# One chunk of LN2's modulation on GpSimd, the shared chunk last in Wo, two K steps moved up, fewer warm-ups: a DiT block on one core

## The chip, the cores and the metric

The kernel runs on one core of a Trainium2 chip (trn2). The metric is the device time of one execution in microseconds (us). The kernel before took 244.13 us, the median of three executions (243.96 to 244.31). An execution counts as slow when it is over 1.5% longer than the fastest of the same kernel; all others are called fast, and only fast ones are compared. In what follows PE is TensorE (the matmul engine), ACT is ScalarE, DVE is VectorE, POOL is GpSimd and SP is SyncE, which issues most DMAs.

## The reference

A DiT block with modulated layer norms, attention with two heads of 576 and a four-fold MLP, all in bfloat16.

```python
B, N, D, F = 2, 256, 1152, 4608
mod = (silu(c) @ w_mod).reshape(B, 6, 1, D)
shift_a, scale_a, gate_a, shift_m, scale_m, gate_m = [mod[:, i] for i in range(6)]
h = layernorm(x) * (1 + scale_a) + shift_a
q, k, v = split(h @ wqkv)                      # H = 2, Dh = 576
a = softmax(q @ k.T * Dh ** -0.5) @ v          # per head
x = x + gate_a * (a.reshape(B, N, D) @ wo)
h2 = layernorm(x) * (1 + scale_m) + shift_m
return x + gate_m * (gelu(h2 @ w_fc1) @ w_fc2)
```

The 512 tokens are four tiles of 128 (tiles 0 and 1 are batch 0, tiles 2 and 3 batch 1). D is nine chunks of 128 columns. A head has four and a half chunks, so chunk 4 (`HC = Dh // P`) is shared by the two heads.

## The kernel before

Four places matter. Each engine gets its instructions in the order in which the program writes them, which is the order here. `P` is 128, `N` the 256 tokens of a batch, `T` all 512; `KM1` is 6. The "K stage" below is the K projection with what feeds it.

The start. PE has nothing real to do until x has been normalised, so it multiplies zeros ("warm-ups") to get its clock up (in the trace of before the step from one to the next falls from 427 to 216 ns). Then it transposes normalised x, computes `scale_a` in four groups of columns (`scale_group`, waits for parts of `w_mod`), has ACT or DVE multiply the transposed x by it (`modulate`), and starts the K projection one contraction chunk at a time (`k_step`), on whichever tiles are ready.

```python
def k_step(k, c0=0, c1=T):              # six output chunks, contraction chunk k, tokens c0:c1
    for m in range(KM1):
        ...
        nc.tensor.matmul(pk[m][:, c0:c1], w_k[:, k, m * P:(m + 1) * P], hT0[:, k, c0:c1], ...)

warm(18, pwarm)                         # after 4 earlier ones
act_stats(ACT.Identity, dsum)
...
norm1(0, 0, CUT, "d")                   # tile 0 normalised, by DVE
pt_0 = transpose_x([0, 1], [0])
warm(3, pwarm)
...
scale_group(0)("a")                     # PE: scale of chunks 0, 1; ACT: + 1
for k in range(2): modulate(pt_0, k, k, 0, 0, P, "a")
warm(1, pwarm)
pt_1 = transpose_x([0, 1], [1])
for k in range(2): modulate(pt_1, k, k, 1, 0, P, "d")
...
pt_2 = transpose_x([0, 1], [2])
for k in range(2): modulate(pt_2, k, k, 2, 0, P, "a")
scale_group(1)("a")
sqrt1(3); recip1(3)
norm1(3, 0, CUT, "d")                   # tile 3 normalised
pt_3 = transpose_x([2, 3], [0, 1])
for i, k in enumerate((2, 3)): modulate(pt_3, i, k, 0, 0, N, "a")
k_step(0, N, N + P)                     # tile 2's first K steps
k_step(1, N, N + P)
pt_4 = transpose_x([0, 1], [3])
for k in range(2): modulate(pt_4, k, k, 3, 0, P, "d")
k_step(2, 0, N)
k_step(3, 0, N)
...
pt_5 = transpose_x([2, 3], [2, 3])
```

The loads that feed this part are issued in this order by SP, right behind x.

```python
KGROUPS = [(0, 2), (2, 4), (4, 6), (6, 9)]
for k0, k1 in KGROUPS:
    nc.sync.dma_start(w_scale_a[:, :, k0 * P:k1 * P], wmod_v[...])    # scale weights of the group
    for k in range(k0, k1):
        nc.sync.dma_start(w_k[:, k, 0:KM1 * P], wqkv_v[...])          # K weights, chunk by chunk
```

The Wo projection contracts over the nine chunks of `aT`, which ACT and DVE have just copied from PSUM; the shared chunk 4 is copied last (`pv_shared`).

```python
for k in range(KD):                     # KD = 9
    nc.tensor.matmul(pacc[:], aT[:, k, t * P:(t + 1) * P], w_o[:, k, c0:c1], start=(k == 0), stop=(k == KD - 1))
```

LN2's modulation works in place on `hT`, which a transposing DMA writes. FC1 (`w_f1`) of batch 0 starts on it chunk by chunk.

```python
def ln2_modulate(b, ks=range(KD)):
    for k in ks:
        h = hT[:, k, b * N:(b + 1) * N]
        if b == 0 or k % 3 == 2:
            nc.scalar.activation(h, h, ACT.Identity, bias=shift_m[...], scale=scale_m[...])
        else:
            nc.vector.tensor_scalar(h, h, scale_m[...], shift_m[...], op0=ALU.mult, op1=ALU.add)
...
wo_group(3, 0)
ln2_modulate(0, range(6))
ln2_stats(2, 2)
ln2_sqrt(2)
ln2_modulate(0, range(6, KD))
wo_group(3, 1)
...                                     # then FC1
```

Of the kernel before, what the change touches and what calls it, by code (L numbers as in the profile page):

```python
# [11 lines left out]
ALU = mybir.AluOpType  # L12
# [7 lines left out]
def kernel(  # L20
# [11 lines left out]
    nc = tc.nc  # L32
    B, N, D = x.shape
# [3 lines left out]
    P = 128  # L37
# [3 lines left out]
    KD = D // P  # L41
# [17 lines left out]
    def acc_tile(shape, name, dt=FP32):  # L59
        return psum.tile(shape, dt, name=name, tag="acc", bufs=6)  # L60

    def aux_tile(shape, name, dt=FP32):
        return psum.tile(shape, dt, name=name, tag="aux", bufs=2)
# [95 lines left out]
    HC = Dh // P  # L159
# [4 lines left out]
    pwarm = acc_tile([P, T], "pwarm")  # L164


    def warm(n, dst):
        for _ in range(n):
            nc.tensor.matmul(dst[:], zeros[:, 0:P], zeros[:], start=True, stop=True)  # L169
# [30 lines left out]
    def act_stats(f, dst):  # L200
        nc.scalar.activation(
            xns[T_ACT][:], x_sb[:, T_ACT, :], f, bias=pivot, scale=-1.0, accum_out=dst[:],
        )

    def act_stats_finish():
        nc.vector.scalar_tensor_tensor(
            dm2[:], dsum[:], -1.0 / (D * D), dsum[:], op0=ALU.mult, op1=ALU.mult
        )
        nc.vector.scalar_tensor_tensor(
            mv1[:, T_ACT, 1:2], dsq[:], 1.0 / D, dm2[:], op0=ALU.mult, op1=ALU.add  # L210
        )
        nc.vector.scalar_tensor_tensor(
            mv1[:, T_ACT, 0:1], dsum[:], -1.0 / D, pivot, op0=ALU.mult, op1=ALU.add
        )
# [4 lines left out]
    def recip1(t, with_nb=False):  # L219
        nc.vector.reciprocal(rstd1[:, t:t + 1], rstd1[:, t:t + 1])  # L220
        if with_nb:
            nc.vector.scalar_tensor_tensor(
                nb1[:, t:t + 1], mv1[:, t, 0:1], -1.0, rstd1[:, t:t + 1], op0=ALU.mult, op1=ALU.mult
            )

    def norm1(t, c0, c1, eng):
        if eng == "a":
            nc.scalar.activation(
                xns[t][:, c0:c1], x_sb[:, t, c0:c1], ACT.Identity,
                bias=nb1[:, t:t + 1], scale=rstd1[:, t:t + 1],  # L230
            )
        else:
            nc.vector.tensor_scalar(
                xns[t][:, c0:c1], x_sb[:, t, c0:c1], mv1[:, t, 0:1], rstd1[:, t:t + 1],
                op0=ALU.subtract, op1=ALU.mult,
            )
# [23 lines left out]
    def transpose_x(ks, ts, pt=None, js=None):  # L260
        pt = aux_tile([P, len(ks), len(ts) * P], "pt", BF16) if pt is None else pt
        for i, k in enumerate(ks):
            for j, t in enumerate(ts) if js is None else zip(js, ts):
                nc.tensor.transpose(pt[:, i, j * P:(j + 1) * P], xns[t][:, k * P:(k + 1) * P], ident[:])
        return pt

    def modulate(pt, i, k, t0, j0, w, eng):
        b = t0 // TPB
        dst, src, sc = hT0[:, k, t0 * P:t0 * P + w], pt[:, i, j0:j0 + w], scale_a[:, k, b:b + 1]
        if eng == "d":  # L270
            nc.vector.tensor_scalar_mul(dst, src, sc)
        else:
            nc.scalar.mul(dst, src, sc)
# [8 lines left out]
    def k_step(k, c0=0, c1=T):  # L282
        for m in range(KM1):
            if k == 0 and c0 == 0:
                pk[m] = acc_tile([P, T], "pk")
            nc.tensor.matmul(  # L286
                pk[m][:, c0:c1], w_k[:, k, m * P:(m + 1) * P], hT0[:, k, c0:c1],
                start=(k == 0 and c0 == 0), stop=(k == KD - 1), skip_group_check=True,
            )
# [36 lines left out]
    s_rows = work.tile([P, KD, SW], BF16, name="s_rows", tag="s_rows", bufs=1)  # L326

    CUT = 4 * P
    warm(18, pwarm)
    act_stats(ACT.Identity, dsum)  # L330
    for j in range(NPD):
        stats_piece(0, j)
# [4 lines left out]
    norm1(0, 0, CUT, "d")  # L337
    stats_piece(2, 1)
    pt_0 = transpose_x([0, 1], [0])
    warm(3, pwarm)  # L340
    act_stats_finish()
    sqrt1(T_ACT)
    stats_piece(2, 2, False)
# [24 lines left out]
    sqrt1(3)  # L368
    recip1(3)
    norm1(3, 0, CUT, "d")  # L370
    pt_3 = transpose_x([2, 3], [0, 1])
    for i, k in enumerate((2, 3)):
        modulate(pt_3, i, k, 0, 0, N, "a")
    k_step(0, N, N + P)
    k_step(1, N, N + P)
    pt_4 = transpose_x([0, 1], [3])
    for k in range(2):
        modulate(pt_4, k, k, 3, 0, P, "d")
# [33 lines left out]
    def vec_section(stat, w, name, nk=KD):  # L412
        pn = aux_tile([P, nk * 32], "pn")
        for k in range(KD):
            wk4 = w[:, k, :].rearrange("p (j q r) -> p q j r", q=4, r=32)
            for i in range(4):
                nc.tensor.matmul(
                    pn[32 * i:32 * i + SW, :].rearrange("p (j r) -> p j r", r=32),
                    stat[:, k, :], wk4[:, i, :, :],
                    start=(k == 0), stop=(k == KD - 1), tile_position=(0, 32 * i),  # L420
                )
        dst = act.tile([P, nk, 32], FP32, name=name)
        nc.vector.transpose(dst[:].rearrange("p k c -> p (k c)"), pn[:])
        return dst
# [59 lines left out]
    scale_m = act.tile([P, KD, B], FP32, name="scale_m")  # L484
# [8 lines left out]
    for k in range(KD):  # L493
        for m in range(KM1):
            nc.tensor.matmul(  # L495
                pq[m][:], w_q[:, k, m * P:(m + 1) * P], hT[:, k, :],
                start=(k == 0), stop=(k == KD - 1),
            )
    for m in range(KD):
        if m >= KM1:  # L500
            pq.append(acc_tile([P, T], "pacc"))
            for k in range(KD):
                nc.tensor.matmul(
                    pq[m][:], w_q[:, k, m * P:(m + 1) * P], hT[:, k, :],
                    start=(k == 0), stop=(k == KD - 1),
# [10 lines left out]
    for b in range(B):  # L516
        for h in range(H):
            scores[b, h] = acc_tile([P, TPB, N], "ps_s")
            for qt in range(TPB):
                q0 = b * N + qt * P  # L520
                for i in range(HC):
# [3 lines left out]
                        start=(qt == 0 and i == 0), stop=False, skip_group_check=True,  # L525
                    )
    for b in range(B):
        for qt in range(TPB):
            q0 = b * N + qt * P
            for h in range(H):  # L530
# [3 lines left out]
                    start=False, stop=True, skip_group_check=True, tile_position=(h * HP, 0),  # L534
# [128 lines left out]
    def ln2_modulate(b, ks=range(KD)):  # L663
        for k in ks:
            h = hT[:, k, b * N:(b + 1) * N]
            if b == 0 or k % 3 == 2:
                nc.scalar.activation(  # L667
                    h, h, ACT.Identity, bias=shift_m[:, k, b:b + 1], scale=scale_m[:, k, b:b + 1],
                )
            else:  # L670
                nc.vector.tensor_scalar(
                    h, h, scale_m[:, k, b:b + 1], shift_m[:, k, b:b + 1], op0=ALU.mult, op1=ALU.add,
                )
# [5 lines left out]
    def wo_group(t, i):  # L679
        b = t // TPB  # L680
        c0, c1 = cuts[t][i:i + 2]
        pacc = acc_tile([P, c1 - c0], "pacc")
        for k in range(KD):
            nc.tensor.matmul(  # L684
                pacc[:], aT[:, k, t * P:(t + 1) * P], w_o[:, k, c0:c1],
                start=(k == 0), stop=(k == KD - 1),
            )
        tmp = work.tile([P, c1 - c0], FP32, name="tmp", tag="tmp", bufs=3)
        nc.vector.tensor_tensor(tmp[:], pacc[:], gate_a[:, b, c0:c1], op=ALU.mult)  # L689
        (nc.vector if (t, i) in ((1, 2), (3, 3)) else nc.gpsimd).tensor_tensor(  # L690
            x1[:, t, c0:c1], tmp[:], x_sb[:, t, c0:c1], op=ALU.add
        )

    def ln2_stats(t, i):
        c0, c1 = cuts[t][i:i + 2]
        nc.vector.bn_stats(stats2[t][:, i, :], x1[:, t, c0:c1])

    wo_group(0, 0)
    wo_group(0, 1)
    ln2_stats(0, 0)  # L700
    wo_group(0, 2)
    ln2_stats(0, 1)
    wo_group(1, 0)
# [19 lines left out]
    shift_m = vec_section(sT, w_shift_m, "shift_m")  # L723
# [4 lines left out]
    ln2_stats(2, 1)  # L728
# [6 lines that stand above are left out]
    ln2_stats(3, 0)  # L735
# [52 lines left out]
    for b in range(B):  # L788
        for m0 in range(0, MSPLIT, 2):
            ms = range(m0, min(m0 + 2, MSPLIT))  # L790
            pacc = acc_tile([P, len(ms), N], "pacc")
            for m in ms:
                for k in range(KD):
                    f1_mm(pacc[:, m - m0, :], m, k, b * N, (b + 1) * N)
            if b == 0 and ms[-1] == MSPLIT - 3:
                ln2_modulate(1)
            nc.scalar.activation(gT[:, ms[0]:ms[-1] + 1, b * N:(b + 1) * N], pacc[:], ACT.Gelu_apprx_tanh)  # L797
# [41 lines left out]
    for gi, (n, t, c0, cw) in enumerate(groups):  # L839
        b = t // TPB  # L840
        last = gi == len(groups) - 1
        pacc = acc_tile([P, cw], "pacc")
        for kk in range(KF):
# [4 lines left out]
                start=(kk == 0), stop=(kk == KF - 1),  # L848
# [51 lines left out]
```

## Time and profile before

| what | before |
|---|---|
| median of 3 executions | 244.13 us |
| profiled span | 242.5 us |
| PE busy | 237.0 us, 98% |
| sum of PE's losses in the K stage, 9.7 to 14.3 us | 1.4 us |
| loss in the first Wo group | 0.14 us |
| loss at the start of FC1 | 0.52 us |

From the page of the kernel before, two rows of the table of engines (busy us, share of the span, instructions) and the first line of the chain of waits that ended last:

```profile
PE 237.0 (98%) x1703; PEld 143.4 (59%) x1703; DVE 93.2 (38%) x207; ACT 70.7 (29%) x141; POOL 31.3 (13%) x47
PE 58%; ACT 2%; DMA 1%; issue 0%; DVE 0%; ACTq 0%; DVEq 0%
```

PE is the engine that counts. But 98% busy doesn't mean that it lost nothing in between. Matmuls overlap in the trace, so the end of one covers the start of the next (the profile's page lists those of Wo at 314 ns in the mean, while one of 384 columns starts every 163). The Trainium skill warns of the busy share in "Perfetto Trace Analysis", section "Identifying the Most-Contended Engine": it is not a good measure of how close to its peak TensorE runs, because its instructions are pipelined. That 98% also hides waits is what this trace adds. The view of PE's waits names few of them (who waited for whom: us in total, times, longest us):

```profile
PE pwarm L169 <- DVE eps_t L92: 1.2, 1, 1.2
PE pt L264 <- ACT big L273: 0.3, 1, 0.3
PE pacc L781 <- ACT hT L667: 0.2, 1, 0.2
```

Apart from the start it names 0.5 us. Subtracting from each matmul's start the start of the one before, and comparing that with the step of an unhindered stream in this trace (216 ns for 512 columns, 163 for 384, 109 for 256, 56 for 128), finds 2.1 us: 1.4 in the K stage, 0.14 in Wo, 0.52 at FC1. (Ten switches from one kind of matmul to another, of 0.09 to 0.11 us each, are left out.) This count of lost step time is what the rest of the document uses. (A few matmul records are missing from a trace; they show as exactly two steps and are not losses.)

The K stage in the timeline of before (start us, length us, engine, line, operation, out<-in, how many in a row, idle before and what ended it; some lines between are left out here and in the fences below):

```profile
3.14 5.54 PE L169 MATMUL pwarm<-zeros 128*128 128x512 bf16 x18
8.52 0.28 PE L264 MATMUL pt<-ident,xn 128*128 128x128 bf16 x2
9.28 0.59 PE L246 MATMUL pm<-sT,w_scale_a 128*128 128x2 bf16 x18
10.60 0.47 DVE L271 TENSOR_SCALAR big<-pt,scale_a 128x128 bf16<-128x128 bf16 x2 [1.46 <-ACT big L273]
13.12 0.38 PE L264 MATMUL pt<-ident,xn 128*128 128x128 bf16 x4 [0.29 <-ACT big L273]
13.34 0.83 PE L286 MATMUL pk<-big,w_k 128*128 128x128 bf16 x12
13.82 0.41 DVE L233 TENSOR_SCALAR xn<-x_sb,mv,rstd 128x512 bf16<-128x512 bf16 x1
14.29 0.28 PE L264 MATMUL pt<-ident,xn 128*128 128x128 bf16 x2
14.41 1.47 PE L286 MATMUL pk<-big,w_k 128*128 128x256 bf16 x12
```

The transposes of tile 0 (8.52) come straight after the last warm-up; their input had been ready since 7.14. The first scale group follows at 9.28; its weights had landed at 8.77. At 13.12 the transposes `pt_3` wait for ACT, then tile 2's K steps run (13.34), and then `pt_4` starts at 14.29, just after DVE has normalised tile 3 (13.82 + 0.41).

The start of Wo and of FC1 in the same timeline:

```profile
77.07 9.10 PE L684 MATMUL pacc<-w_o,big 128*128 128x384 bf16 x54
77.23 0.58 ACT L298 CAST big<-pa 128x512 bf16<-128x512 f32 x1 [0.47 <-PE pa L619]
94.51 3.06 ACT L667 ACTIVATE hT<-hT,shift_m,scale_m 128x256 bf16<-128x256 bf16 x6 [3.41 <-DMA hT<-xn]
97.65 1.57 ACT L667 ACTIVATE hT<-hT,shift_m,scale_m 128x256 bf16<-128x256 bf16 x3
97.88 1.17 PE L781 MATMUL pacc<-hT,w_f 128*128 128x256 bf16 x8
99.27 3.98 PE L781 MATMUL pacc<-hT,w_f 128*128 128x256 bf16 x35 [0.22 <-ACT hT L667]
```

Chunk 4's copy ends at 77.81, while the fifth matmul of Wo could have run at 77.73. ACT gets the nine chunks of batch 0 done at 99.22; FC1 wants the eighth at 98.64 and the ninth 0.11 us later.

### The profile page before, as it was taken

The numbers are of one execution on the slowest core, as the hardware profiler recorded it, in microseconds if no ns is written. First come the engines' busy times: TensorE is split into PE (matmuls) and PEld (weight loads), VectorE is DVE, ScalarE is ACT, GpSimd is POOL, SyncE is SP. The second block draws the span as 40 slices with busy tenths as digits, with TensorE's granted clock in tenths as the row PEclk, the third lists the DMA queues.
The fourth block names the chain that finished last, engine by engine and source line by source line (L and its number), as shares of the span: only waits on it lengthen the run. The fifth ranks groups of instructions, "written<-read, shape, count | busy, mean of one in ns | idle before, by whom it ended". The sixth has DMA issues, their size and how long they took to land.

```text
span 242.5 us, 4040 instructions
## 1 busy us (share of the span) xinstructions
PE 237.0 (98%) x1703; PEld 143.4 (59%) x1703; DVE 93.2 (38%) x207; ACT 70.7 (29%) x141; POOL 31.3 (13%) x47
## 2 busy tenths in 40 slices
PE   8999999999999999999999999999999999999994
PEld 2586444466656566888854444444665666566573
DVE  3762550665694676720000029999001000000001
ACT  6542250543736074872222223332000000000000
POOL 1012000000310516200000000000314111111111
PEclk9999999999999999999999999999999999999999
DMA  7999999999999998789999999997981000000000
GB/s 238 329 334 343 383 356 224 351 367 275 256 322 364 377 248 213 188 193 332 328 328 254 212 232 326 327 327 220 281 255 35 16 16 16 19 19 27 21 17 16
DMA packets 76989, 54.48 MB, mean 225 GB/s; under 512 B 26011, under 2 KB 72491, under 8 KB 76971
## 3 DMA queue, kind: packets, MB, share of 16 engines
q1 hardware_dynamic: 76240, 53.02, 77.4%
q0 software_dynamic: 704, 1.20, 1.6%
q8 instruction: 13, 0.21, 0.4%
q14 instruction: 5, 0.04, 0.0%
q10 hardware_dynamic: 27, 0.00, 0.0%
HBM read 46.90 MB, written 1.19 MB: 198 GB/s over the span
## 4 chain that ended last, share of the span: by engine, by line
PE 58%; ACT 2%; DMA 1%; issue 0%; DVE 0%; ACTq 0%; DVEq 0%
PE pacc L845 29%; PE pacc L781 29%; ACT hT L667 2%; DMA hT<-xn 1%; ACT xn L650 0%; ACT rstd L641 0%; DVE tmp L851 0%; DVE o_sb L853 0%; ACTq L667 0%; DVEq L851 0%
## 5 line engine op out<-in xcount | busy, mean ns | idle before, releaser
L781 PE MATMUL pacc<-hT,w_f 128*128 128x256 bf16 (+1 forms) x432 | 70.7, 326 | 0.2 <-ACT hT L667 0.2
L845 PE MATMUL pacc<-w_f,gT 128*128 128x384 bf16 (+2 forms) x468 | 70.5, 314 | 0.0
L845 PEld LDWEIGHTS <-gT 128*128 128x128 bf16 x468 | 44.4, 98 | 26.2
L781 PEld LDWEIGHTS <-w_f 128*128 128x128 bf16 x432 | 42.2, 98 | 28.2 <-issue 0.5
L469 DVE SCALAR_TENSOR_TENSOR late<-w_gate_mT,late 128x1152 bf16<-128x1152 bf16 x18 | 24.4, 1357 | 36.8 <-DMA w_gate_mT<-in_w_mod_dram 36.2
L851 DVE TENSOR_TENSOR tmp<-pacc,gate 128x384 f32<-128x384 f32 (+2 forms) x13 | 6.8, 526 | 63.0 <-PE pacc L845 51.3
L819 ACT ACTIVATE gT<-pacc 128x512 bf16<-128x512 f32 x24 | 14.3, 597 | 32.3 <-PE pacc L781 32.3
L469 DVE SCALAR_TENSOR_TENSOR s_spill<-w_scale_m,s_b 128x1152 bf16<-128x1152 bf16 x12 | 16.3, 1357 | 8.3 <-DMA w_scale_m<-in_w_mod_dram 8.0
L684 PE MATMUL pacc<-w_o,big 128*128 128x384 bf16 (+2 forms) x117 | 18.1, 314 | 0.0
L568 PE MATMUL pacc<-w_v,hT 128*128 128x384 bf16 x108 | 17.9, 326 | 0.0
L853 POOL TENSOR_TENSOR o_sb<-tmp,x 128x384 bf16<-128x384 f32 (+1 forms) x12 | 11.6, 972 | 48.1 <-DVE tmp L851 48.1
L684 PEld LDWEIGHTS <-big 128*128 128x128 bf16 x117 | 10.9, 98 | 7.0 <-ACT big L298 0.4
L568 PEld LDWEIGHTS <-hT 128*128 128x128 bf16 x108 | 10.4, 98 | 7.0 <-issue 0.2
L286 PE MATMUL pk<-big,w_k 128*128 128x128 bf16 (+2 forms) x102 | 13.4, 279 | 0.1
L690 POOL TENSOR_TENSOR x<-tmp,x_sb 128x384 f32<-128x384 f32 (+1 forms) x11 | 9.8, 889 | 18.0 <-DVE tmp L689 9.3
L495 PE MATMUL pacc<-hT,w_q 128*128 128x512 bf16 x54 | 11.8, 379 | 0.0
L324 POOL DMA_DIRECT2D gates_dram<-grow x4 | 2.0, 514 | 70.6 <-DVE grow L805 70.6
L797 ACT ACTIVATE gT<-pacc 128x512 bf16<-128x512 f32 x12 | 6.9, 597 | 10.8 <-PE pacc L781 10.8
L169 PE MATMUL pwarm<-zeros 128*128 128x512 bf16 x26 | 8.6, 486 | 1.2 <-DVE eps_t L92 1.2
L286 PEld LDWEIGHTS <-w_k 128*128 128x128 bf16 x102 | 7.8, 98 | 3.1 <-issue 0.2
L495 PEld LDWEIGHTS <-w_q 128*128 128x128 bf16 x54 | 5.3, 98 | 6.4
L689 DVE TENSOR_TENSOR tmp<-pacc,gate 128x384 f32<-128x384 f32 (+2 forms) x13 | 6.7, 522 | 5.5 <-PE pacc L684 5.4
(98 smaller groups left out, 160.2 us busy)
## 6 DMA issues: line engine op xcount, KB each, us to landing
w_f<-in_w_fc_dram SPq DMA_DIRECT2D x14, 864.0 KB, 10.9
w_f<-in_w_fc_dram SPq DMA_DIRECT2D x2, 2592.0 KB, 10.3
w_f<-in_w_fc_dram SPq DMA_DIRECT2D x2, 1728.0 KB, 14.5
w_shift_a<-in_w_mod_dram SPq DMA_DIRECT2D x3, 864.0 KB, 11.0
w_v<-in_wqkv_dram SPq DMA_DIRECT2D x3, 864.0 KB, 6.0
w_gate_a<-in_w_mod_dram SPq DMA_DIRECT2D x3, 864.0 KB, 9.1
w_o<-in_wo_dram SPq DMA_DIRECT2D x3, 864.0 KB, 6.0
w_shift_m<-in_w_mod_dram SPq DMA_DIRECT2D x3, 864.0 KB, 13.0
```

Source lines behind the costliest of these rows:

```text
L169: nc.tensor.matmul(dst[:], zeros[:, 0:P], zeros[:], start=True, stop=True)
L286: nc.tensor.matmul(pk[m][:, c0:c1], w_k[:, k, m * P:(m + 1) * P], hT0[:, k, c0:c1], start=(k == 0 and c0 == 0), stop=(k == KD - 1), skip_g ...
L469: nc.vector.scalar_tensor_tensor(spill, wT[:, j, :], 1.0, s_b[b], op0=ALU.mult, op1=ALU.mult, accum_out=dst(j, b),)
L495: nc.tensor.matmul(pq[m][:], w_q[:, k, m * P:(m + 1) * P], hT[:, k, :], start=(k == 0), stop=(k == KD - 1),)
L568: nc.tensor.matmul(pacc[:], hT[:, k, t * P:(t + 1) * P], w_v[:, k, pnl * PW:(pnl + 1) * PW], start=(k == 0), stop=(k == KD - 1),)
L684: nc.tensor.matmul(pacc[:], aT[:, k, t * P:(t + 1) * P], w_o[:, k, c0:c1], start=(k == 0), stop=(k == KD - 1),)
L690: (nc.vector if (t, i) in ((1, 2), (3, 3)) else nc.gpsimd).tensor_tensor(x1[:, t, c0:c1], tmp[:], x_sb[:, t, c0:c1], op=ALU.add)
L781: nc.tensor.matmul(dst, w_f1[m // KD][:, k, ml * P:(ml + 1) * P], hT[:, k, c0:c1], start=(k == 0), stop=(k == KD - 1),)
L797: nc.scalar.activation(gT[:, ms[0]:ms[-1] + 1, b * N:(b + 1) * N], pacc[:], ACT.Gelu_apprx_tanh)
L819: nc.scalar.activation(gT[:, m, :], pacc[:], ACT.Gelu_apprx_tanh)
L845: nc.tensor.matmul(pacc[:], gT[:, kk, t * P:(t + 1) * P], w_f2[j][:, r, c0 - n * PW:c0 - n * PW + cw], start=(kk == 0), stop=(kk == KF - 1),)
L853: (nc.vector if last else nc.gpsimd).tensor_tensor(o_sb[:], tmp[:], x1[:, t, c0:c0 + cw], op=ALU.add)
```

## The change

Four small things. Fewer warm-ups should let the transposes of tile 0 start when their input is ready. Tile 2's first K steps go ahead of the transposes `pt_3`, to fill PE's wait at 13 us. The shared chunk goes last in Wo's contraction, so that its copy has time. The last chunk of batch 0's LN2 modulation goes from ACT to POOL, so that the chain of nine on ACT becomes eight.

```diff
-    warm(18, pwarm)
+    warm(12, pwarm)
...
     pt_0 = transpose_x([0, 1], [0])
-    warm(3, pwarm)
+    warm(4, pwarm)
...
     norm1(3, 0, CUT, "d")
+    k_step(0, N, N + P)
+    k_step(1, N, N + P)
     pt_3 = transpose_x([2, 3], [0, 1])
     for i, k in enumerate((2, 3)):
         modulate(pt_3, i, k, 0, 0, N, "a")
-    k_step(0, N, N + P)
-    k_step(1, N, N + P)
     pt_4 = transpose_x([0, 1], [3])
...
-            if b == 0 or k % 3 == 2:
+            if b == 0 and k == KD - 1:
+                nc.gpsimd.tensor_scalar(
+                    h, h, scale_m[:, k, b:b + 1], shift_m[:, k, b:b + 1], op0=ALU.mult, op1=ALU.add,
+                )
+            elif b == 0 or k % 3 == 2:
                 nc.scalar.activation(
...
-        for k in range(KD):
+        ks = [k for k in range(KD) if k != HC] + [HC]
+        for k in ks:
             nc.tensor.matmul(
                 pacc[:], aT[:, k, t * P:(t + 1) * P], w_o[:, k, c0:c1],
-                start=(k == 0), stop=(k == KD - 1),
+                start=(k == ks[0]), stop=(k == ks[-1]),
```

## The prediction

> **What bounds it now.** TensorE. The page gives PE 237.0 of 242.5 us busy (98%), and the chain of waits is two PE stages, FC1 and FC2 (29% each), reached through ACT modulations of batch 0's LN2. Busy hides small stalls, so I compared the starts of successive matmuls with their streaming step (216 ns for 512 columns, 109 for 256, 56 for 128). Apart from the cold start and fixed switches of about 0.1 us, PE loses time in three places only:
> - K stage, 9.7 to 14.3 us: five waits, 0.27+0.29+0.16+0.43+0.28 = 1.4 us, for ACT and DVE results.
> - First Wo group, 77.7 us: chunk 4 waits 0.14 us for the shared chunk's ACT copy (77.23 to 77.81).
> - FC1 start, 98.6 to 99.3 us: chunks 7 and 8 wait 0.14+0.38 us for ACT, which modulates nine chunks in line, about 0.5 us each, after the transposing DMA landed at 94.40.
>
> After 14.3 us PE is fed without further stalls, and the DMA landings I checked have 0.7 us or more of slack, so time won early should reach the end.
>
> **Warm-ups.** In the timeline their step is 427 ns until 6.1 us, then 216: seven of the 18 are cold. The Trainium skill, "TensorE: Matmul & The Clock Gate", Part 1, says the ramp is a time of activity (about 3.4 us), not a count; this trace agrees roughly (matmuls from 1.2 us, warm at 6.1). So the six removed are warm: 6 x 0.216 = 1.3 us, and one added back, 0.2. But the first transposes then run at 7.2 instead of 8.5 us, and the modulation products behind them need the first scale weights, which land at 8.77 us. They start now at 9.28, so they can move to about 8.85: a gain of 0.35 to 0.4, not 1.1. About 0.6 us of new PE idle appears before them. The next scale group has its weights at 11.85 (used at 12.2), just early enough.
>
> **K steps ahead of the transposes.** They fill the 0.43 us wait. But from 10.6 us the chain that ends last is DVE: modulate, statistics, normalize of tile 3 (10.60 to 14.23), then the transposes at 14.29. PE only waits sooner or later for it. Worth about 0 by itself (-0.1 to +0.15).
>
> **Shared chunk last.** The first Wo group reads chunk 4 at 8 x 0.163 = 1.3 us after its start, well after the copy. Gain 0.14.
>
> **Chunk 8 on GpSimd.** It leaves the ACT queue (0.5 us less) and runs on POOL between two additions, about 96.7 us. POOL's two-input 128x384 addition takes 0.91 us; the skill's "GPSIMD Engine Reference", section 4.1, calls one-input work roughly line-rate; no such instruction is in this trace. I estimate 0.4 to 0.8 us, done before 97.6, needed at 98.7. The 0.38 wait goes; chunk 7's 0.14 stays, since ACT's start and PE move together. Gain 0.38.
>
> **Sum.** 0.37 + 0 + 0.14 + 0.38 = 0.9 us: 244.13 becomes **243.2 us**, 80% range 242.8 to 243.65. Faster by over 2%: 0.005; within 2%: 0.985; slower by over 2%: 0.01.
>
> **Right if:** pt_0's transposes near 7.2 us; scale group 0 waits on its DMA and starts near 8.85; tile 3's transposes near 13.9; no wait inside the first Wo group; FC1's last-chunk wait on ACT gone with one of about 0.14 at chunk 7; K stage done about 0.4 us earlier.
>
> **Wrong if:** the clock warms later in the new schedule or drops again in the new idle gap (slower by 1 us or more); the scale weights land earlier or later than profiled (each 0.1 us counts fully until the K stage); GpSimd's instruction takes over 2 us; or the reordered K steps push the next transposes and ACT's modulations past the DVE chain (losing 0.1 to 0.3 us).

## The result, and the profile after

The kernel after took 243.77 us, the median of six executions (243.33 to 243.90), against 244.22 us for six of the kernel before (243.96 to 245.03). The ratio is 0.9973 with a 95% interval of 0.9956 to 0.9990. Ratios here are the mean time of one kernel's fast executions over that of the other's in the same rounds, so not quite the ratio of the medians quoted. In mean times the change won 0.66 us; a repeat (below) won 0.79. For scale: the kernel before, run against itself, "won" 0.28 us in the same way (b_again).

The profiled span went from 242.5 to 242.1 us. PE's waits in the view of after:

```profile
PE pwarm L169 <- DVE eps_t L92: 1.2, 1, 1.2
PE pm L246 <- DMA w_scale_a<-in_w_mod_dram: 0.7, 2, 0.4
PE pt L264 <- DVE xn L233: 0.4, 1, 0.4
```

The waits for ACT have gone, and waits for the loads of `w_scale_a` have come. The K stage in the timeline of after:

```profile
7.19 0.29 PE L264 MATMUL pt<-ident,xn 128*128 128x128 bf16 x2
8.75 0.60 PE L246 MATMUL pm<-sT,w_scale_a 128*128 128x2 bf16 x18 [0.41 <-DMA w_scale_a<-in_w_mod_dram]
12.35 0.83 PE L286 MATMUL pk<-big,w_k 128*128 128x128 bf16 x12
13.01 0.39 PE L264 MATMUL pt<-ident,xn 128*128 128x128 bf16 x4
13.50 0.84 ACT L273 ACTIVATE big<-pt,scale_a 128x256 bf16<-128x256 bf16 x2 [0.42 <-PE pt L264]
13.77 0.29 PE L264 MATMUL pt<-ident,xn 128*128 128x128 bf16 x2 [0.38 <-DVE xn L233]
14.02 1.47 PE L286 MATMUL pk<-big,w_k 128*128 128x256 bf16 x12
20.21 0.83 PE L246 MATMUL pm<-sT,w_scale_a 128*128 128x2 bf16 x27 [0.32 <-DMA w_scale_a<-in_w_mod_dram]
```

The transposes start at 7.19 instead of 8.52, but the first scale group only at 8.75 instead of 9.28: it waits for its weights, which landed at 8.70. (The second group, at 11.86, starts 0.04 after its weights too. That costs nothing here: `pt_4` comes as long after the first group as in before.) `pt_4` is at 13.77, 0.52 earlier; the K step behind it at 14.02, 0.39 earlier. Then, at 20.21, the fourth scale group waits for weights that landed at 20.16 (18.88 in the trace of before). PE loses 0.49 us of step time there and comes out of it 0.10 later than before. In this one execution the early gain was gone by 20 us.

The start of Wo and of FC1:

```profile
77.23 8.95 PE L689 MATMUL pacc<-w_o,big 128*128 128x384 bf16 x54
94.53 3.06 ACT L671 ACTIVATE hT<-hT,shift_m,scale_m 128x256 bf16<-128x256 bf16 x6 [3.42 <-DMA hT<-xn]
96.67 0.55 POOL L667 TENSOR_SCALAR hT<-hT,scale_m,shift_m 128x256 bf16<-128x256 bf16 x1
97.68 1.07 ACT L671 ACTIVATE hT<-hT,shift_m,scale_m 128x256 bf16<-128x256 bf16 x2
97.88 5.34 PE L786 MATMUL pacc<-hT,w_f 128*128 128x256 bf16 x46
```

Wo's 54 matmuls of batch 0 take 8.95 us instead of 9.10. FC1 starts at 97.88 in both traces (0.16 late into Wo, 0.15 won there), and no longer has a break after eight matmuls: the lost step time at its start is 0.16 instead of 0.52 us. POOL's chunk took 0.55 us and was done at 97.22.

So the net of this trace, 0.34 us, is the late parts alone. Two questions follow. Does the change itself make the fourth scale group's weights late, or was that this execution? And what are the two early parts worth?

### The profile page after: what moved, and what is told of

Its sections match the earlier page's. It is cut to its first block, busy times and chain, and to the rows that moved or that the text cites. A ratio compares the mean times of both kernels' runs of the same rounds, so it can differ in the third digit from the quotient of the medians.

```text
span 242.1 us, 4022 instructions
## 1 busy us (share of the span) xinstructions
PE 235.7 (97%) x1689; PEld 142.8 (59%) x1698; DVE 93.2 (38%) x207; ACT 70.3 (29%) x140; POOL 31.9 (13%) x48
## 4 chain that ended last, share of the span: by engine, by line
PE 90%; SPq 4%; DMA 4%; issue 0%; DVE 0%; DVEq 0%
PE pacc L850 29%; PE pacc L786 29%; PE pacc L689 7%; PE pacc L568 7%; PE pacc L495 5%; DMA w_scale_a<-in_w_mod_dram 4%; SPq L109 3%; PE pk L315 2%; PE pacc L503 2%; PE pk L286 2%; PE pa L603 1%; PE ps_s L523 1%; PE pn L417 1%; SPq L104 1%; PE pg L451 1%
## 5 line engine op out<-in xcount | busy, mean ns | idle before, releaser
L169 PE MATMUL pwarm<-zeros 128*128 128x512 bf16 x21 | 7.4, 503 | 1.2 <-DVE eps_t L92 1.2
```

Source lines behind the costliest of these rows:

```text
L169: nc.tensor.matmul(dst[:], zeros[:, 0:P], zeros[:], start=True, stop=True)
```

## The experiments

Two theories were put against each other first. A: the change makes the fourth load late, and the early parts are worth nothing. B: that landing wanders, and the early parts have a gain of their own. The runs of one round share a chip: the first eight ran on one, warm24 and warm8 on a second, warm_only_2 and best_2 on a third.

### The kernel before again (b_again)

No edit. Expected:

> The kernel before once more, unchanged, for the noise and for a second look at the landing of the fourth group of scale weights (the last of the four loads of w_scale_a; 18.88 us in the first trace of before, 20.16 in that of after). Ratio expected 1.000 within 0.002. Theory A (the change itself delays that landing): it lands near 18.9 again and TensorE does not wait for it. Theory B (the landing wanders from execution to execution by about 1.3 us): it may land anywhere from 18.9 to 20.2, and if after 19.9 TensorE waits for it here too.

Measured: 0.9987 (0.9964 to 1.0010) over four executions, so an equal pair differs by over 0.1% here. The profiled execution was the slowest of the four (244.89 us, the others 244.0). In its timeline:

```profile
3.14 6.16 PE L169 MATMUL pwarm<-zeros 128*128 128x512 bf16 x18
9.89 0.59 PE L246 MATMUL pm<-sT,w_scale_a 128*128 128x2 bf16 x18
```

The same 18 warm-ups took 6.16 instead of 5.54 us, since the clock came up at 7.6 instead of 6.4 us (that is where the step falls to 216 ns), and the first scale group started at 9.89, 0.95 after its weights had landed (8.94). Everything behind it is 0.6 us later to the end: the span is 243.1 us. So the length of the warm-up stretch is not fixed, and it goes straight into the time. The fourth group landed at 19.24, and there was no wait for it.

### The kernel after again (a_again)

No edit. Expected:

> The kernel after once more, unchanged. Ratio expected 0.997 to 0.9985 (-0.4 to -0.7 us). Theory A: the fourth scale group lands near 20.2 us again and TensorE waits about 0.5 us for it. Theory B: it may land near 18.9, and then the whole trace is about 0.4 us shorter, near 241.7 us.

Measured: 0.9967 (0.9947 to 0.9987), just under the range, median 243.66 against 244.35 us. The fourth group landed at 19.45 and was not waited for. Theory A falls here: the same kernel without the late landing. What made it late in the first trace, no run shows. The time from the third landing to the fourth was 5.28 us there and 3.66 to 4.42 in the eleven other traces with the same order of loads (the slow one of warm_only among them), old and new schedules alike. A weaker form of A, that fewer warm-ups make a late landing likelier, stays open: it came in one of seven traces with 12 or 8 warm-ups and in none of five with 18 or 24.

### The late parts alone (late_only)

```diff
 (the K stage as before)
+        ks = [k for k in range(KD) if k != HC] + [HC]        # Wo: shared chunk last
+            if b == 0 and k == KD - 1: nc.gpsimd.tensor_scalar(...)   # chunk 8 on GpSimd
```

Expected:

> The two late parts alone (shared chunk last in Wo, chunk 8 on GpSimd), K stage as before. If they add up as read from the traces: 0.14 + 0.37 us less, ratio near 0.998. If Wo's 0.14 us is given back at the FC1 start: 0.37 us, ratio 0.9985. Under theory A this alone already makes all that the change gains.

Measured: 0.9977 (0.9960 to 0.9994), 0.53 us less in the mean. That fits the sum of 0.51, but the interval doesn't exclude 0.37. The trace decides for Wo: from Wo's first matmul to FC1's first it is 20.65 us, and 20.81 in all six fast traces with the old order. All seven traces with the new order have 20.65. So Wo's 0.15 is kept.

This execution's clock came up early (5.1 us), and the old 18 warm-ups were over in time. The scale group waits for its weights here too:

```profile
3.20 4.83 PE L169 MATMUL pwarm<-zeros 128*128 128x512 bf16 x18
9.24 0.60 PE L246 MATMUL pm<-sT,w_scale_a 128*128 128x2 bf16 x18 [0.46 <-DMA w_scale_a<-in_w_mod_dram]
```

In such an execution the removal of warm-ups can win next to nothing. (This execution itself gained nothing over the first trace of before, 242.5 us in both: its transposing DMA landed later, see the last table.)

### The early parts alone (k_only)

```diff
+    warm(12, pwarm) ... warm(4, pwarm)
+    k_step(0, N, N + P); k_step(1, N, N + P)       # ahead of pt_3
 (Wo and LN2's modulation as before)
```

Expected:

> The two early parts alone (warm-ups 12 and 4, K steps of tile 2 first), the late parts as before. Theory A: the fourth scale group lands near 20.2 us, the 0.4 us won by 18.4 us are lost to the wait for it, ratio 1.000 (0.0 to +0.1 us). Theory B: mean gain between 0 and 0.4 us, ratio 0.998 to 1.000, with the landing varying.

Measured: 0.9988 (0.9970 to 1.0006), 0.27 us less in the mean; no wait for the fourth group (landed at 19.23). This sits in the middle of theory B's range. It can't be told from zero by the times alone, so the two early parts were taken apart.

### Only the warm-up counts (warm_only, warm_only_2)

Expected:

> Only the warm-up counts changed (18 to 12, 3 to 4). Theory C (the warm-ups cost time only where they end after the first scale weights land, and that depends on when the clock warms, 4.8 to 7.6 us in the five traces so far): the first scale group starts within 0.1 us of that landing whatever the warming time, and the way from it to the transposes of columns 2 and 3 of tiles 2 and 3 (the fifth transposing group, 15.72 us in before) stays 6.44 us as in the three traces with the old order. Mean gain over before about 0.3 to 0.45 us, ratio 0.998 to 0.999, larger in those executions of before where the clock warms late. Rival (the fewer warm-ups leave the clock cold longer): [...]ratio above 1.001.

Measured: 0.9982 (0.9966 to 0.9998) over five executions. The sixth, the profiled one, took 277.56 us at a granted clock of 0.85; it is left out. Expected of the repeat:

> warm_only once more, because its profile fell in an execution at a granted clock of 0.85. Expected: first scale group within 0.1 us of the landing of its weights, 6.44 us from there to the fifth transposing group, ratio 0.997 to 0.999 as in its five fast runs (0.9982).

Measured, on the third chip: 1.0003 (0.9987 to 1.0020). That is a miss: no gain in five executions. (The means differ by 0.02 us in its favour, the ratio by rounds by 0.03% against it; both are zero within the noise.) The trace was as expected: the first scale group started 0.05 us after the landing of its weights, and the distance to `pt_5` is 6.45 us. Taken together the times leave the warm-ups' mean gain between zero and half a microsecond; the traces say when it is there.

### Only the order of the K steps (reorder_only)

Expected:

> Only the K steps of tile 2 moved ahead of the transposes of columns 2 and 3. Theory D (the reorder costs): the way from the first scale group to the fifth transposing group is 6.57 us instead of 6.44, because the moved-back transposes delay ACT's modulation and K step 2 waits 0.12 us for it; ratio 1.0000 to 1.001 (0.13 us slower in the mean, below what the times resolve). Rival (the reorder gains 0.1 to 0.4 us, as intended): that way is 6.0 to 6.35 us.

Measured: 1.0001 (0.9985 to 1.0018), no change that the times resolve. The trace shows what the reorder does:

```profile
12.65 0.83 PE L286 MATMUL pk<-big,w_k 128*128 128x128 bf16 x12
13.31 0.39 PE L264 MATMUL pt<-ident,xn 128*128 128x128 bf16 x4
13.80 0.84 ACT L273 ACTIVATE big<-pt,scale_a 128x256 bf16<-128x256 bf16 x2 [0.42 <-PE pt L264]
14.08 0.29 PE L264 MATMUL pt<-ident,xn 128*128 128x128 bf16 x2 [0.38 <-DVE xn L233]
14.32 1.47 PE L286 MATMUL pk<-big,w_k 128*128 128x256 bf16 x12
```

The K steps fill the wait, and the wait comes back in front of `pt_4` (14.08), where PE needs DVE's normalised tile 3. Meanwhile `pt_3` is later than it was, so ACT begins its two modulations later (13.80), and the K step behind `pt_4` waits 0.12 us for the first of them.

### The change without the reorder (no_reorder)

Expected:

> The kernel after with the order of the K steps put back. Theory D: 0.13 us faster than after in the same trace distance (6.44 us), ratio to before about 0.996 to 0.9975. Rival (the reorder helps together with the other parts): ratio 0.9975 or more, distance above 6.57.

Measured: 0.9964 (0.9949 to 0.9979), median 243.53 us; distance 6.45 us. Here the clock came up later than in any other trace (7.7 us), and the first scale group still started at 8.90. That is 0.34 after its weights had landed, so "within 0.1 us whatever the warming time", as expected of warm_only, doesn't hold at the latest clock. The kernel before, with the clock up at 7.6 us, started it at 9.89. The intervals of no_reorder and after overlap, so that the reorder costs 0.12 us is shown by the traces, not by the times.

```profile
12.74 0.38 PE L264 MATMUL pt<-ident,xn 128*128 128x128 bf16 x4 [0.20 <-ACT big L273]
13.22 0.84 ACT L273 ACTIVATE big<-pt,scale_a 128x256 bf16<-128x256 bf16 x2
13.92 0.28 PE L264 MATMUL pt<-ident,xn 128*128 128x128 bf16 x2
14.04 1.47 PE L286 MATMUL pk<-big,w_k 128*128 128x256 bf16 x12
```

With the old order PE waits before `pt_3`, ACT has its input in time, and the K step follows `pt_4` at once.

### More and fewer warm-ups (warm24, warm8)

```diff
-    warm(18, pwarm)          # kernel before
+    warm(24, pwarm)          # warm24
-    warm(12, pwarm)          # no_reorder
+    warm(8, pwarm)           # warm8
```

Expected of warm24:

> The kernel before with 24 instead of 18 warm-ups. Theory C (the first scale group starts at the later of two things: the landing of its weights, or the end of the warm-ups): now the warm-ups end last whatever the warming time, so all six added ones count at full: the first scale group starts 10.0 to 11.3 us, about 1.2 us later than before in the mean, and the whole kernel is 1.0 to 1.4 us longer, ratio 1.004 to 1.006. Rival (the start of the K stage is bound elsewhere, and the warm-ups only fill its time): ratio below 1.002.

Measured: 1.0051 (1.0038 to 1.0064), 1.28 us more. Six warm steps of 0.216 are 1.30. In the trace the first scale group started at 9.96, just under the range, and 1.07 after its weights, with the clock up as early as 5.1 us:

```profile
3.13 6.23 PE L169 MATMUL pwarm<-zeros 128*128 128x512 bf16 x24
9.96 0.59 PE L246 MATMUL pm<-sT,w_scale_a 128*128 128x2 bf16 x18
```

Expected of warm8:

> no_reorder with 8 instead of 12 warm-ups. Theory C: the weights' landing (8.6 to 9.1 us) already ends the wait with 12, so four fewer gain nothing more: first scale group within 0.1 us of the landing, ratio to before 0.9955 to 0.997 as for no_reorder. If the clock warms later for want of work in some executions (about 0.6 us idle before the first transposes instead of none): [...]a wider spread of times, ratio 0.997 to 1.001.

Measured: 0.9976 (0.9957 to 0.9994): no further gain over no_reorder, and by the letter outside theory C's range and inside that of its rival. The group started 0.04 us after the landing (8.40 after 8.36, the earliest of all). The executions spread wider (243.29 to 244.78) than those of no_reorder (243.44 to 243.87). The trace fell in one where the clock was up by 4.3 us, so none shows the one at 244.78. But the record gives it a mean granted clock of 0.993, where every other fast execution has 0.997 to 1.000. A lack of 0.7% of 243 us is 1.7 us at full clock, or 3.4 us at half (0.5 is the lower clock in the traces): an estimate, which fits a clock that fell back or came late, as the rival has it. The other five average 243.61. So eight warm-ups gain nothing more, and that they are as safe as 12 is not shown.

### A version with two more changes (best, best_2)

```diff
 (no_reorder, and)
     for k0, k1 in KGROUPS:
-        load scale weights of the group
+        if k0 < 6: load scale weights of the group
         for k in range(k0, k1):
             load w_k[:, k]
+            if k == 4: load scale weights of the fourth group
...
-            if b == 0 and k == KD - 1:       # GpSimd
+            if b == 0 and k >= 6:            # GpSimd
```

Expected:

> no_reorder, with the last group of scale weights loaded one K chunk of w_k earlier (issued before the K weights of chunk 5) and chunks 6, 7 and 8 of batch 0's modulation on GpSimd. If the late landing of the fourth scale group in the first trace of after was the chance loss that I take it for, that group now has 0.5 us more of slack and is never waited for; if the wait at the FC1 start hangs on when the transposing DMA lands (0.16 to 0.71 us in the five traces), it falls to 0 to 0.2 us. Expected 0.3 to 0.5 us below no_reorder at least in the trace, ratio to before 0.995 to 0.9965, and never an execution above 244.0 us. Against it: GpSimd's three chunks (0.55 us each) hold back its additions for tile 3, which would show as a wait at the start of FC1's second batch; expected 0.

Measured: 0.9957 (0.9940 to 0.9974), median 243.31 against 244.52 us. Once more, on the third chip, expected:

> best once more, for its ratio (0.9957, interval 0.9940 to 0.9974) and to see whether the fourth scale group and the first batch's FC1 start are free of waits in a second trace. Expected ratio 0.995 to 0.9965; no wait above 0.1 us at either place unless the transposing DMA lands more than 0.5 us later than in the first trace of before against the start of FC1.

Measured: 0.9953 (0.9940 to 0.9965), median 243.06 against 244.31 us. In both traces the fourth group's weights landed 1.1 us before they were used (18.49 for 19.59; 18.32 for 19.47), and FC1's first matmuls run without a lost step:

```profile
94.41 3.06 ACT L677 ACTIVATE hT<-hT,shift_m,scale_m 128x256 bf16<-128x256 bf16 x6 [3.98 <-DMA hT<-xn]
95.99 1.63 POOL L673 TENSOR_SCALAR hT<-hT,scale_m,shift_m 128x256 bf16<-128x256 bf16 x3
97.20 3.00 PE L792 MATMUL pacc<-hT,w_f 128*128 128x256 bf16 x26
```

POOL's additions for tile 3 go on at 97.59, 0.39 after FC1's first matmul (at 97.24 and 0.64 before it in after), and no wait at FC1's second batch comes of it. From FC1's first matmul to the last matmul of the kernel it is 140.43 us in both, 140.59 in after and 140.95 in before: the differences are the lost steps at FC1's start (0, 0.16, 0.52), so what is won there reaches the end. That best beats before is clear; its interval overlaps those of after and no_reorder, and its two additions were not run apart. The earlier load made no trace worse; the one late landing happened in one trace of twelve with the old order of loads, so two traces don't prove that it is cured.

### The traces side by side

The K stage. "Clock up" is the start of the first warm-up that comes under 0.30 us after the one before. Distances are from the first scale group's first matmul. All times in us, worked out from the starts of matmuls and the landings in each trace (the slow trace of warm_only is left out).

| trace | warm-ups | K steps | clock up | first weights land | first scale group | to `pt_4` | to `pt_5` |
|---|---|---|---|---|---|---|---|
| before | 18 | old | 6.36 | 8.77 | 9.28 | 5.01 | 6.44 |
| b_again | 18 | old | 7.62 | 8.94 | 9.89 | 5.02 | 6.45 |
| late_only | 18 | old | 5.06 | 9.20 | 9.24 | 5.02 | 6.45 |
| warm24 | 24 | old | 5.10 | 8.89 | 9.96 | 5.01 | 6.44 |
| reorder_only | 18 | moved | 5.93 | 8.88 | 9.06 | 5.02 | 6.57 |
| after | 12 | moved | 6.24 | 8.70 | 8.75 | 5.02 | 6.58 |
| a_again | 12 | moved | 5.89 | 9.04 | 9.08 | 5.02 | 6.57 |
| k_only | 12 | moved | 4.76 | 9.06 | 9.11 | 5.02 | 6.58 |
| warm_only_2 | 12 | old | 5.37 | 8.84 | 8.89 | 5.02 | 6.45 |
| no_reorder | 12 | old | 7.71 | 8.56 | 8.90 | 5.02 | 6.45 |
| warm8 | 8 | old | 4.26 | 8.36 | 8.40 | 5.02 | 6.45 |
| best | 12 | old | 5.06 | 8.69 | 8.74 | 5.02 | 6.46 |
| best_2 | 12 | old | 5.41 | 8.57 | 8.61 | 5.03 | 6.46 |

The start of FC1: lost step time against how long before FC1's first matmul the second transposing DMA of batch 0 landed.

| chunks on GpSimd | landed 3.39 to 3.48 us before | landed 2.90 to 3.17 us before |
|---|---|---|
| none | 0.52 (before), 0.54 (b_again), 0.53 (reorder_only), 0.54 (warm_only_2) | 0.83 (k_only), 0.92 (warm24) |
| chunk 8 | 0.16 (after), 0.16 (a_again), 0.23 (no_reorder) | 0.71 (late_only), 0.57 (warm8) |
| chunks 6 to 8 | 0 (best_2) | 0 (best) |

## Why the prediction was right or wrong

The direction, the class and roughly the size were right: predicted 0.93 us less, measured 0.66 and 0.79 less in two sets of means, with intervals of about 0.4 us to either side. The ratio 0.9973 applied to the 244.13 us on which the prediction rested is 243.47 us, inside its range; the bare median, 243.77, is 0.12 above it, as the kernel before also ran a little slower in that set. Point by point:

- **Warm-ups: the mechanism was right, the term was taken from one execution.** "They start now at 9.28, so they can move to about 8.85: a gain of 0.35 to 0.4". In the trace the first scale group moved to 8.75, bound by its weights' landing, with the new idle time in front of it as foretold. But 0.37 is no constant. The group starts at the later of the landing and the end of the warm-ups. With 18 the end moved with the clock: 9.89 in b_again, already in time in late_only. With 12 the start followed the landing in every trace but one, where the clock was latest, and there it was still 0.99 earlier than b_again's. So the term is 0 to 1 us per execution. In the mean of the traces the group started 0.42 us after the landing with 18 (four traces) and 0.09 with 12 (seven), a gain of 0.33; that the one execution's 0.37 came so near to it is luck. On times it measured 0.48 less (warm_only) and 0.02 less (warm_only_2, another chip). warm24 shows the other side: added warm-ups count in full, 1.28 for a computed 1.30. The Trainium skill, "TensorE: Matmul & The Clock Gate", Part 1, says that the window is free-running and the cold count varies from run to run, and cautions against fitting to it. The prediction cited that page for the length of the ramp and then fitted to one count all the same. These traces agree with the free-running window of 3.413 us: the clock came up between 4.26 and 7.71 us, a spread of 3.45 us, and in their clock records full clock lasts either 235.52 or 238.93 us in every fast trace, 3.41 apart. They do not agree with the ±500 ns that the page gives for the transition.
- **K steps ahead of the transposes: the reason was right, the size a little off.** "Worth about 0 by itself (-0.1 to +0.15)". It costs 0.12 to 0.13 us, in every one of four traces (6.57 or 6.58 against 6.44 to 6.46). The first half of the argument holds: `pt_4` comes 5.01 to 5.03 us after the first scale group with either order, since DVE's chain sets it, so filling the wait wins nothing. The second half was listed only under "wrong if": the later transposes push ACT's modulation past `pt_4`, and K step 2 waits 0.12 us for it. In the trace of after ACT begins at 13.50 and its first result is there at 13.97, while K step 2, due 0.12 after `pt_4` at 13.89, starts at 14.02.
- **Shared chunk last: right.** 0.14 predicted, 0.15 or 0.16 measured in seven traces, and not given back.
- **Chunk 8 on GpSimd: right.** 0.38 predicted; 0.52 to 0.16 is 0.36. The instruction took 0.55 us, inside the estimate of 0.4 to 0.8. The 0.14 that "stays" was 0.16. What wasn't foreseen is that the wait hangs on the transposing DMA's landing as well: 0.3 to 0.6 us later makes it 0.57 to 0.71 even with the chunk moved, against 0.83 to 0.92 without, so in such executions the gain is only 0.1 to 0.35.
- **Slack after the K stage: the step that failed in the profiled execution.** "The DMA landings I checked have 0.7 us or more of slack, so time won early should reach the end." The fourth scale group had 1.2 us of slack in the trace of before (18.88 for 20.11). In the trace of after it landed 1.28 later and was needed 0.4 earlier, and 0.49 us were lost, more than the early gain. Slack read from one trace is a sample, not a bound. In the eleven other traces with that order of loads it was in time, so it didn't cost the mean much; what made it late stays open.

The terms as measured add up: 0.15 (Wo) + 0.36 (GpSimd) + 0 to 1 (warm-ups) - 0.12 (reorder) is 0.4 to 1.4 us; with the traces' mean of 0.33 for the warm-ups it is about 0.7, near the 0.66 and 0.79 of the times. In the profiled execution the late landing took the early part away and 0.34 was left. So of the predicted 0.93 the reorder's cost of 0.12 is the largest part that is missing in the mean; GpSimd's smaller gain after a late landing and the rare late load take more from single executions.

## What to carry to other kernels

A filler in front of real work costs its full time as soon as it ends last (six more warm-ups: 1.28 us for a computed 1.30), so set it by what the work behind it waits for (here a DMA landing) and by the worst execution, not by one trace; 12 warm-ups held the start within 0.05 us of the landing in six of seven traces and within 0.34 in the one with the latest clock; 18 left 0.04 to 0.95. Fewer is not always better: eight gained nothing more, and one of six executions had a lower clock. Before filling an engine's idle gap, ask whether another engine's chain ends after the gap anyway: then the filler only moves the gap, and whatever the filler pushes back can become the new wait. When a step hangs on a chain of equal pieces on one engine, spreading the last pieces over an idle engine can take away both the mean wait and its dependence on when the input lands (three of nine chunks on GpSimd: no lost step in two traces whose landings lay 0.56 us apart).

## What the Trainium skill lacked or had wrong

- "TensorE: Matmul & The Clock Gate", Part 1: right on the two step times (427 and 216 ns in these traces) and on the free-running window (clock up from 4.26 to 7.71 us after the start). Its ±500 ns for the transition is too narrow for these traces, which spread over 3.45 us. It lacks the cost of warming up too long. A warm-up matmul issued in front of real work counts in full once it ends last: six more made the kernel 1.28 us longer, and with 18 the K stage's first product started 9.06 to 9.89 us after the start, depending on when the clock came up, with 12 at 8.61 to 9.11.
- "GPSIMD Engine Reference", section 4.1: calls one-input elementwise work roughly line-rate. A `tensor_scalar` of 128x256 bf16 with two per-partition scalars took 552 ns on POOL, 343 ns on DVE and 587 ns on ACT (mean of one; back to back 0.54 on POOL and about 0.51 on ACT). At the 1.2 GHz of the page's section 1, "Specifications", that is an estimate of 2.6 cycles an element with the fixed cost in it; one size was run, so the two are not separated, and the page's statement is neither confirmed nor refuted. The section gives no time for such an instruction.
- "Perfetto Trace Analysis", section "Identifying the Most-Contended Engine": right that matmul busy time misleads (98% busy hid 2.1 us of lost steps here). What it lacks is that the overlap of matmuls also hides waits: the gaps that the view names after the start sum to 0.5 us here, and comparing successive matmul starts with the unhindered step found 2.1.
- No page looked up gives the spread of a load's landing between executions of one program: the first group of scale weights, issued at 1.66 us in every trace, landed between 8.36 and 9.20 us, and the fourth once 1.3 us later than in the trace of before.
